# Second layer of a two-layer mixture of experts: one weight conversion behind the low halves, the second job's place lookup behind its next half of products

## The chip, the cores and the metric

The kernel runs on one core of one Trainium2 chip. The metric is device time in microseconds of the whole program, the median of the runs. In the profile the engines are PE (TensorE matrix products), PEld (its weight loads), DVE (VectorE), ACT (ScalarE), POOL (GpSimd) and SP (SyncE, here the queue of the weight loads).

## The reference

A retention layer (blockwise attention with decay) gives 1536 tokens of 512 values. Two mixtures of experts follow, each with 8 experts of 512 -> 1024 -> 512. The first sends every token to two experts with noisy gates; the second, which the change touches, to one:

```python
logits = x @ w_gate
expert_idx = np.argmax(logits, axis=1)
...
for i in range(N):
    e = expert_idx[i]
    if counts[e] < capacity:
        disp[e, counts[e]] = x[i]
        pos[i] = counts[e]
        counts[e] += 1
        keep[i] = True
h = np.maximum(np.einsum('ecd,edf->ecf', disp, w1), 0.0)
y = np.einsum('ecf,efd->ecd', h, w2)
for i in range(N):
    if keep[i]:
        out[i] = gate_w[i] * y[expert_idx[i], pos[i]]
```

Here the capacity is 384 and everything is float32.

## The kernel before

Each layer is a list of jobs. A job is an expert with a number of token places: the second layer has a first job S of 256 places and a second job T of 128 places for the same expert (the largest), then the other experts by size, the next one with 336 places. For a job the tokens' rows are gathered from DRAM by POOL (L529, indirect DMA), POOL adds their two parts (the join, L540), PE transposes them (L860), ACT and DVE split them into a high and a low half (L861, L862), and PE multiplies.

A float32 product is made of three products of halves (`three`, L870 to L872): high x high, high x low, low x high. So every weight part of 128 x 1024 is converted too: ACT makes the high half (L108, `convert`), DVE the low half (L114, `convert_low`), after which its landing buffer is free for the next load from SP (`places`). The converted parts stand in rings of four for each matrix.

Job T has only 128 places, so it is worked "by token" in four steps (`steps`): two halves of the first product (`first_rows`; ACT's relu at L979 follows each), then the transposed activations of a half (`turn`: PE at L987, ACT's high half at L990, DVE's low half at L991) and the second product. The first half of the second product is `highs_first` (L1024), which takes all products with high halves before those with low halves; the rest is `second` (L870 to L872). `turn(0)` is recorded inside `first_rows(1)`, `turn(1)` inside step 2.

For every place the kernel must also know its gate weight and its target row. `one_hot` finds them with products of a one-hot matrix (L402), a copy (L404), a transposition (L407) and some small DVE operations (L408 to L426: `far` L424, the weight `wt` L426, the target `dst` L425). For S and T the first two columns are looked up early and the rest by `rest()`, named `jobS.rest` and `jobT.rest`; the ranked lookup for all later jobs is `later[1][7]` (L483, L505). The outputs of a job are scaled by the weight (ACT at L1110, DVE at L1108) and scattered (L1117).

`experts` walks through jobs and steps. After each step it records what runs beside it: conversions, the next job's gather and split (`nxt.ready()`), and `extra2(j, i)`, hand-written work for job j, step i. `sooner` lists the steps at which `extra2` comes ahead of the conversions. The order of each engine's instructions is made from this recording and from `tc.issue_after(...)`, which orders an instruction behind a named one; `tail` holds the last instruction of a kind. At job 1 (T):

```python
if j == 1 and i == 0:
    with tc.issue_after(tail["pe"]):
        jobS.rest()
        later[1][7]()
    places.append(more[2])
if j == 1 and i == 1:
    with tc.issue_after(tail["pe"]):
        jobT.rest()
    with tc.issue_after(tail["dve"]):
        st2 = sizes_by_expert(...)
        later.append(leftovers(...))
```

`leftovers` counts the tokens that found no place (L1187 to L1197, with `sizes_by_expert` at L361 to L367); a branch four jobs later reads the count.

Of the kernel before, what the change touches and what calls it, by code (L numbers as in the profile page):

```python
# [8 lines left out]
F32 = mybir.dt.float32  # L9
# [28 lines left out]
def kernel(ctx: ExitStack, tc: tile.TileContext, q, k, v, lam, g1, gn, noise,  # L38
                                  w1, w2, g2, u1, u2, capacity, out):
    nc = tc.nc  # L40
    B, H, S, D = q.shape
    T, DM = out.shape
    E, _, F = w1.shape
# [20 lines left out]
    def bank(tag, shape, dt=F32):  # L64
        bufs = 2 if tag in ("hp", "tr") else 1
        return psum.tile(shape, dt, name=tag, bufs=bufs)
# [6 lines left out]
    tail = {}  # L73
# [9 lines left out]
    def fetch():  # L83
        if not wq or not places:
            return
        key, layer, j, src = wq.pop(0)
        st = places.pop(0)
        if layer == 0:
            a = src[:, j * 256:(j + 1) * 256].rearrange("(c p) f -> p c f", p=P)
            i = nc.sync.dma_start(st.rearrange("p (c f) -> p c f", c=DC), a)  # L90
        else:
            a = src[j * 256:(j + 1) * 256, :].rearrange("(c p) d -> p c d", p=P)
            i = nc.sync.dma_start(st.rearrange("p (c d) -> p c d", c=2), a)
        tail["sp"] = i.ins
        while hold:
            tc.add_manual_dep(i.ins, hold.pop().name, mybir.DependencyInfo(
                mybir.DependencyClass.Sync, mybir.DependencyReason.DATA), reason="loads behind a gather")
        staged.append((key, layer, j, st))

    def convert():  # L100

        if not staged or split_[staged[0][1]] - used[staged[0][1]] == RING:
            return
        key, layer, j, st = staged.pop(0)
        at = split_[layer] % RING
        hi, lo = wh[layer][at], wl[layer][at]
        split_[layer] += 1
        tail["cast"] = nc.scalar.copy(hi, st).ins  # L108
        lows.append(((key, layer, j), hi, lo, st))

    def convert_low():
        if lows:
            part, hi, lo, st = lows.pop(0)
            tail["low"] = nc.vector.tensor_sub(lo, st, hi.bitcast(F32)).ins  # L114
            wparts[part] = (hi, lo)
            places.append(st)
# [40 lines left out]
    i = nc.sync.dma_start(lam1, lam.rearrange("(o h) -> o h", o=1))  # L157
# [25 lines left out]
    ps = bank("yp3", [P, H])  # L183
# [690 lines left out]
    class Job:  # L874
# [107 lines left out]
        def turn(self, m, ahead):  # L982
            r = self.rows
            ps = bank("tr", [P, 4, P])[:, :, :r]
            with tc.issue_after(ahead):
                for i in range(4):
                    nc.tensor.transpose(ps[:, i, :], self.h["r", m][:r, i * P:(i + 1) * P], ident[:r, :r])  # L987
            t = work.tile([P, 2, 512], F32R, name="h", bufs=3).rearrange("p a (b c) -> p a b c", b=4)[:, :, :, :r]
            hh, hl = t[:, 0], t[:, 1]
            nc.scalar.copy(hh, ps)  # L990
            nc.vector.tensor_sub(hl, ps, hh.bitcast(F32))  # L991
            for i in range(4):
                self.h[4 * m + i] = t[:, :, i, :]

# [130 lines left out]
    def experts(jobs, last, extra=None, count=None, between=None, joins=3, sooner=()):  # L1125

        j = 0
        tail.pop("both", None)
        while j < len(jobs) and j != count:
            job = jobs[j]  # L1130
            steps = job.steps()
            for i, step in enumerate(steps):
                for _ in range(0 if job.quiet else 2 if len(steps) == 4 else 1):
                    fetch()
                if job.pairs and i == 1:
                    convert_low()
                step()
                nxt = jobs[j + 1] if j + 1 < len(jobs) else None
                if i == len(steps) - 1 and j + 1 < len(jobs) and j + 1 != count:
                    job.collect()  # L1140
                if i == job.clears and last is not None:
                    last.collect()
                    last.finish()
                    if j == 0 and between is not None:
                        between()
                if i == 1 and nxt is not None:
                    nxt.prepare()
                if nxt is not None and i >= (1 if job.by_token else joins):
                    nxt.join()
                if i == 6 and j + 2 < len(jobs) and nxt.by_token:  # L1150
                    jobs[j + 2].prepare()
                tail.pop("cast", None)
                tail.pop("low", None)
                sooner_cast = nxt is not None and nxt.pairs and job.by_token and i == 2
                if sooner_cast:
                    with tc.issue_after(tail["act"]):
                        convert()
                if i == len(steps) - 2 and nxt is not None:
                    nxt.ready()
                if extra is not None and (j, i) in sooner:  # L1160
                    extra(j, i)
                with tc.issue_after(tail["act"]), tc.issue_after(tail["dve"]):
                    if job.pairs or sooner_cast:
                        while lows:
                            convert_low()
                    for _ in range((2, 2, 0 if sooner_cast else 1, 1)[i] if job.by_token else (2, 1, 1, 1, 1, 1, 1, 0, 0)[i] if job.pairs
                                   else 2 if i < 4 else 1):
                        convert()
                        if not job.pairs:
                            convert_low()  # L1170
                if job.later is not None:
                    with ExitStack() as order:
                        for x in ("act", "dve", "cast", "low"):
                            if x in tail:
                                order.enter_context(tc.issue_after(tail[x]))
                        job.later()
                    job.later = None
                if extra is not None and (j, i) not in sooner:
                    extra(j, i)
            last = job  # L1180
            j += 1
        return last
# [270 lines left out]
    def ahead():  # L1453
# [15 lines left out]
        jobs.append(jobS)  # L1469

    last = experts(jobs, None, extra1, count=len(FIRST) + 2)
    total, body = over1
    with tc.If(total > 0):  # L1473
# [85 lines left out]
    def extra2(j, i):  # L1559
        if j == 0 and i == 2:  # L1560
            route2()
            jobT.src, jobT.dst, jobT.wt, jobT.rest, _, picked = one_hot("D", keyB, aux2, *BEHIND, False, "yp2")
            jobT.g = gather(jobT.src, jobT.n, jobT.rows, x2_rows)
            jobT.join()
            later.append(picked)
        if j == 0 and i == 3:
            with tc.issue_after(later[0]):
                later.append(others())
                jobS.quiet = True
                of, _, pick, spread1, mark = later[1][:5]  # L1570
                pick()
                spread1()
                mark(range(NT))
        if j == 0 and i == 7:
            with tc.issue_after(tail["pe"]):
                later.append(later[1][5]())
                for r in TURNS:
                    jobs.append(Job(("b", r), SECOND[r], later[1][0](r), x2_rows, out, False, SECOND[r][1] > 1, True))
                jobs[2].prepare()
            hold.append(brought[-2])  # L1580
        if j == 0 and i == 7:
            with tc.issue_after(later[3]), tc.issue_after(tail["dve"]):
                gates()
                later[1][6]()
        if j == 1 and i == 0:
            with tc.issue_after(tail["pe"]):
                jobS.rest()
                later[1][7]()
            places.append(more[2])
        if j == 1 and i == 1:  # L1590
            with tc.issue_after(tail["pe"]):
                jobT.rest()
            with tc.issue_after(tail["dve"]):
                st2 = sizes_by_expert("b", later[2], [n for n, _ in SECOND] + [BEHIND[0]])
                later.append(leftovers("b", tab2, table2_full, tot2, st2, x2_rows, u1, u2, out, False))

    jobL = last
    last = experts(jobs, jobL, extra2, count=BEFORE + 2, between=lambda: all_logits(jobL), sooner=((1, 0),))
    def settle(j, i):

# [7 lines left out]
    with tc.If(total > 0):  # L1608
        body()
    last = experts(jobs[BEFORE + 2:], last, settle)  # L1610
    last.collect()
    last.finish()
# [34 lines left out]
```

## Time and profile before

| | |
|---|---|
| median of 3 runs | 598.44 us (598.14 to 599.72) |
| the profiled execution | 600.24 us, its span 598.6 us |
| PE busy | 585.1 us, 98% of the span |
| DVE, ACT, POOL busy | 372.5, 279.8, 182.5 us |
| granted TensorE clock, mean | 0.998 |

Times in the rows are microseconds from the start of the span. A busy PE is not a PE at its peak, since products are pipelined: a product's row is longer than the distance to the next one. Job T lies between 436 and 455 us.

### The profile page before, as it was taken

The numbers are of one execution on the slowest core, as the hardware profiler recorded it, in microseconds if no ns is written. First come the engines' busy times: TensorE is split into PE (matmuls) and PEld (weight loads), VectorE is DVE, ScalarE is ACT, GpSimd is POOL, SyncE is SP. The second block draws the span as 40 slices with busy tenths as digits, with TensorE's granted clock in tenths as the row PEclk, the third lists the DMA queues.
The fourth block names the chain that finished last, engine by engine and source line by source line (L and its number), as shares of the span: only waits on it lengthen the run. The fifth ranks groups of instructions, "written<-read, shape, count | busy, mean of one in ns | idle before, by whom it ended". The sixth has DMA issues, their size and how long they took to land. (4 is left out here: it accounts for less than half of the span.)

```text
span 598.6 us, 11608 instructions
## 1 busy us (share of the span) xinstructions
PE 585.1 (98%) x4305; PEld 555.3 (93%) x4305; DVE 372.5 (62%) x858; ACT 279.8 (47%) x488; POOL 182.5 (30%) x256
## 2 busy tenths in 40 slices
PE   8998989999999999999999999999999999999996
PEld 7997889989999999999999999998879999998996
DVE  5467789766363464543644556546887567667893
ACT  3565530354353343433434435037137367467782
POOL 4965500416023041050130501033165334331204
PEclk9999999999999999999999999999999999999999
DMA  9999415248545357377453520291289967956841
GB/s 183 267 281 264 119 64 190 78 133 298 193 150 185 107 180 229 103 249 211 132 189 105 199 84 30 64 321 61 72 284 338 328 220 217 351 184 215 273 146 35
DMA packets 104869, 109.76 MB, mean 183 GB/s; under 512 B 35700, under 2 KB 80756, under 8 KB 104803
## 3 DMA queue, kind: packets, MB, share of 16 engines
q1 hardware_dynamic: 96722, 83.05, 46.1%
q0 software_dynamic: 8080, 25.88, 12.4%
q8 instruction: 36, 0.59, 0.4%
q14 instruction: 31, 0.25, 0.1%
HBM read 91.89 MB, written 18.71 MB: 185 GB/s over the span
## 5 line engine op out<-in xcount | busy, mean ns | idle before, releaser
L114 DVE TENSOR_TENSOR wl<-wst,wh 128x1024 fp32r<-128x1024 f32 x107 | 134.7, 1267 | 54.6 <-ACT wh L108 49.4
L108 ACT CAST wh<-wst 128x1024 fp32r<-128x1024 f32 x107 | 111.4, 1048 | 33.4 <-PE yp L871 21.8
L870 PE MATMUL hp<-x,wh 128*128 128x364 f32 (+9 forms) x352 | 116.0, 330 | 0.8 <-ACTq L1473 0.4
L871 PE MATMUL hp<-x,wh 128*128 128x364 f32 (+9 forms) x352 | 115.8, 329 | 0.0
L872 PE MATMUL hp<-x,wl 128*128 128x364 f32 (+9 forms) x352 | 114.9, 327 | 0.0
L958 ACT ACTIVATE h<-hp 128x364 fp32r<-128x364 f32 (+9 forms) x88 | 41.2, 468 | 156.2 <-PE hp L872 143.2
L870 PE MATMUL yp<-h,wh 128*128 128x364 f32 (+8 forms) x320 | 106.1, 333 | 0.0
L872 PE MATMUL yp<-h,wl 128*128 128x364 f32 (+8 forms) x320 | 106.0, 332 | 0.0
L871 PE MATMUL yp<-h,wh 128*128 128x364 f32 (+8 forms) x320 | 105.3, 329 | 0.0
L959 DVE SCALAR_TENSOR_TENSOR h<-hp,h 128x364 fp32r<-128x364 f32 (+9 forms) x88 | 46.3, 526 | 60.7 <-ACT h L958 57.5
L1117 POOL DMA_INDIRECT x<-y,Rdst x25 | 24.7, 987 | 176.7 <-DVE y L1091 173.1
L870 PEld LDWEIGHTS hp<-x,wh 128*128 128x128 f32 x352 | 66.1, 188 | 2.0 <-ACTq L1473 0.8
L871 PEld LDWEIGHTS hp<-x,wh 128*128 128x128 f32 x352 | 66.1, 188 | 0.7 <-DVE x L1271 0.2
L872 PEld LDWEIGHTS hp<-x,wl 128*128 128x128 f32 x352 | 66.1, 188 | 0.0
L871 PEld LDWEIGHTS yp<-h,wh 128*128 128x128 f32 x320 | 60.2, 188 | 0.2 <-DVE h L959 0.2
L870 PEld LDWEIGHTS yp<-h,wh 128*128 128x128 f32 x320 | 60.0, 188 | 0.3 <-issue 0.2
L872 PEld LDWEIGHTS yp<-h,wl 128*128 128x128 f32 x320 | 60.1, 188 | 0.0
L862 DVE TENSOR_TENSOR x<-tr,x 128x128 fp32r<-128x128 f32 (+11 forms) x68 | 27.3, 434 | 26.7 <-ACT x L861 25.8
L861 ACT CAST x<-tr 128x128 fp32r<-128x128 f32 (+11 forms) x68 | 24.4, 386 | 32.5 <-PE tr L860 30.2
L540 POOL TENSOR_TENSOR xg<-xg 128x512 f32<-128x512 f32 (+1 forms) x16 | 23.5, 1469 | 43.2 <-DMA xg<-x,Tsrc 28.9
L529 POOL DMA_INDIRECT xg<-x,Rsrc x25 | 29.0, 1158 | 18.4 <-DVE Rsrc L497 11.1
L1082 PE MATMUL tr<-iw,yT 128*128 128x136 f32 (+3 forms) x224 | 34.3, 288 | 0.1
(391 smaller groups left out, 1037.7 us busy)
## 6 DMA issues: line engine op xcount, KB each, us to landing
wst<-in_moe_w_dram SPq DMA_DIRECT2D x107, 512.0 KB
more<-in_moe_w_dram SPq DMA_DIRECT2D x21, 512.0 KB
ldk<-in_k_dram SPq DMA_DIRECT2D x12, 256.0 KB
ldv<-in_v_dram SPq DMA_DIRECT2D x12, 256.0 KB
x<-xr SPq DMA_DIRECT2D x12, 256.0 KB
out_dram<-zero SPq DMA_DIRECT2D x12, 256.0 KB
ldq<-in_q_dram SPq DMA_DIRECT2D x5, 512.0 KB
ldq<-in_q_dram SPq DMA_DIRECT2D x2, 256.0 KB
```

What stands on the lines that cost most here:

```text
L108: tail["cast"] = nc.scalar.copy(hi, st).ins
L114: tail["low"] = nc.vector.tensor_sub(lo, st, hi.bitcast(F32)).ins
L529: i = nc.gpsimd.indirect_dma_start(out=r, out_offset=None, in_=x, in_offset=bass.IndirectOffsetOnAxis(ap=src(s)[:m], axis=0))
L861: a = nc.scalar.copy(hi[:, d, :n], ps[:, :n])
L862: v_ = nc.vector.tensor_sub(lo[:, d, :n], ps[:, :n], hi[:, d, :n].bitcast(F32))
L870: nc.tensor.matmul(ps, a[0], b[0], start=start, stop=False)
L871: nc.tensor.matmul(ps, a[0], b[1], start=False, stop=False)
L872: tail["pe"] = nc.tensor.matmul(ps, a[1], b[0], start=False, stop=stop).ins
L958: tail["act"] = nc.scalar.activation(hh, ps, AF.Relu).ins
L959: tail["dve"] = nc.vector.scalar_tensor_tensor(hl, ps, 0.0, hh.bitcast(F32), op0=OP.max, op1=OP.subtract).ins
L1082: nc.tensor.matmul(ps[:m, i, :], self.yT[:, 2 * b + i, s * r:s * r + m], iw[:, 2 * b + i, gates2], start=True, stop=True)
L1117: i = nc.gpsimd.indirect_dma_start(out=target, out_offset=bass.IndirectOffsetOnAxis(ap=dst, axis=0), in_=y, in_offset=None, bounds_check=t ...
```

## The change

Three edits, all for the second job of the second layer:

```diff
@@ turn
-            nc.vector.tensor_sub(hl, ps, hh.bitcast(F32))
+            tail["low_h"] = nc.vector.tensor_sub(hl, ps, hh.bitcast(F32)).ins
@@ experts
                 tail.pop("low", None)
+                if (j, i - 1) in sooner:
+                    tail["dve"] = tail["low_h"]
...
-                    for _ in range((2, 2, 0 if sooner_cast else 1, 1)[i] if job.by_token else (2, 1, 1, 1, 1, 1, 1, 0, 0)[i] if job.pairs
-                                   else 2 if i < 4 else 1):
+                    casts = ((2, 2, 0 if sooner_cast else 1, 1)[i] if job.by_token else (2, 1, 1, 1, 1, 1, 1, 0, 0)[i] if job.pairs
+                             else 2 if i < 4 else 1)
+                    for c in range(casts):
                         convert()
-                        if not job.pairs:
+                        if not job.pairs and not (c and (j, i) in sooner):
                             convert_low()
@@ extra2
-        if j == 1 and i == 1:
+        if j == 1 and i == 2:
             with tc.issue_after(tail["pe"]):
                 jobT.rest()
+        if j == 1 and i == 1:
             with tc.issue_after(tail["dve"]):
                 st2 = sizes_by_expert("b", later[2], [n for n, _ in SECOND] + [BEHIND[0]])
```

The only step in `sooner` is (1, 0), the first step of job T in the second layer. At that step the low half of the second conversion is no longer recorded. At step 1 `tail["dve"]` is set to the low halves of `turn(0)`, and the conversion's low half and the leftover counts are recorded behind them. `jobT.rest()` moves from step 1 to step 2. The number of instructions is the same on every engine, and SP's queue has the same order. Lines behind L1151 have numbers that are two to four higher after the change.

**DVE, in job T.** The piece from the copy of S's lookup (L404) on; `wl_84` is the low half of the second conversion, `blw` and `bli` belong to the leftover counts, `y` is S's scaled output. Before:

```order
L404 COPY tabi<-tr 4x256
L114 TENSOR_TENSOR wl_84<-wst_73,wh_76 128x1024
L408 COPY Soa<-tr 128x2x4
L505 TENSOR_REDUCE Twt<-yp_5281 128x21
L424 TENSOR_SCALAR Sfar<-Soa 128x2
L426 TENSOR_REDUCE Swt<-Soa 128x2
L1193 TENSOR_REDUCE blw<-blw 128x1
L425 TENSOR_TENSOR Sdst<-Stok,Sfar 128x2
L1197 CAST bli<-blw 128x18
L991 TENSOR_TENSOR h<-tr,h 128x512
L1108 TENSOR_SCALAR y<-yp_4868,Swt 128x512
```

After:

```order
L404 COPY tabi<-tr 4x256
L505 TENSOR_REDUCE Twt<-yp_5281 128x21
L408 COPY Soa<-tr 128x2x4
L424 TENSOR_SCALAR Sfar<-Soa 128x2
L426 TENSOR_REDUCE Swt<-Soa 128x2
L425 TENSOR_TENSOR Sdst<-Stok,Sfar 128x2
L1108 TENSOR_SCALAR y<-yp_4868,Swt 128x512
L991 TENSOR_TENSOR h<-tr,h 128x512
L114 TENSOR_TENSOR wl_84<-wst_73,wh_76 128x1024
L361 MEMSET bsv 128x1 x8
```

The conversion stood between L404 and everything that makes S's weight; now it stands behind the low halves (L991), and the leftover counts, which began among the gate operations earlier, follow it.

**PE, in job T.** The piece around the first products of the second half (L1024); `yp_5349`, `yp_5363` and `ohs` belong to T's lookup. Before:

```order
L402 LDWEIGHTS aux_160
L402 MATMUL yp_5349<-ohs,aux_160 4x128
L1024 MATMUL yp_5403<-wh_79,h 128x512
L407 MATMUL yp_5363<-iw,tabi 128x4
L1024 MATMUL yp_5403<-wl_87,h 128x512
L1024 MATMUL yp_5403<-wh_79,h 128x512
L1024 MATMUL yp_5403<-wl_87,h 128x512
L1024 MATMUL yp_5403<-wh_79,h 128x512 x2
L987 MATMUL tr<-iw,hr 128x128 x4
```

After, the L1024 follow the last product of `first_rows` directly, then L987 and this piece, where `yp_5430` is T's lookup and `xg` are the next job's gathered rows:

```order
L870 MATMUL yp_5383<-wh_80,h 128x512
L871 MATMUL yp_5383<-wl_88,h 128x512
L872 MATMUL yp_5383<-wh_80,h 128x512
L870 MATMUL yp_5383<-wh_80,h 128x512
L871 MATMUL yp_5383<-wl_88,h 128x512
L872 MATMUL yp_5383<-wh_80,h 128x512
L860 MATMUL tr<-iw,xg 128x128 x2
L860 MATMUL tr<-iw,xg 128x80
L860 MATMUL tr<-iw,xg 128x128 x2
L860 MATMUL tr<-iw,xg 128x80
L402 LDWEIGHTS aux_160
L402 MATMUL yp_5430<-ohs,aux_160 4x128
```

T's lookup (twelve L402 and L407) went from ahead of and between the L1024 to behind the first two sets of the next job's transpositions.

**POOL, in job T.** One piece of the difference; `Tsrc` are places of the next jobs, `Sdst` the targets of S:

```order
 L529 DMA xg<-x_67,Tsrc 80x1104
 L540 TENSOR_TENSOR xg<-xg 128x4x128 x2
-L540 TENSOR_TENSOR xg<-xg 80x4x128
-L529 DMA xg<-x_67,Tsrc 128x1104
 L1117 DMA out_dram<-y,Sdst 1536x512 x2
+L540 TENSOR_TENSOR xg<-xg 80x4x128
+L529 DMA xg<-x_67,Tsrc 128x1104
 L540 TENSOR_TENSOR xg<-xg 128x4x128
 L529 DMA xg<-x_67,Tsrc 128x1104 x2
```

The two scatters of S now come ahead of the join of the next job's third tile (80 rows) and of a further gather. On ACT the one row that moves is L1110, the scaling of S's output: it now stands ahead of the first L990 instead of behind it.

## Rows read from the trace of the kernel before

**Rows 1.** The page: busy time of each engine, its share of the span, instructions.
```profile
PE 585.1 (98%) x4305; PEld 555.3 (93%) x4305; DVE 372.5 (62%) x858; ACT 279.8 (47%) x488; POOL 182.5 (30%) x256
```

**Rows 2.** Waits of PE from 400 us on: total us, times, longest us.
```profile
PE yp L1024 <- ACT y L1110: 0.6, 1, 0.6
PE yp L407 <- DVE tabi L404: 0.5, 1, 0.5
```

**Rows 3.** Timeline of PE: start us, us, instruction, idle before and its releaser.
```profile
445.10 0.83 PE L402 MATMUL yp<-ohs,aux 128*4 128x128 bf16 x12
446.55 0.50 PE L1024 MATMUL yp<-wh,h 128*128 128x512 f32 x1 [0.62 <-ACT y L1110]
447.55 0.22 PE L407 MATMUL yp<-iw,tabi 4*128 4x4 f32 x1 [0.49 <-DVE tabi L404]
447.70 0.50 PE L1024 MATMUL yp<-wl,h 128*128 128x512 f32 x1
...
450.81 0.75 PE L860 MATMUL tr<-iw,xg 128*128 128x128 f32 x6
...
452.37 0.47 PE L860 MATMUL tr<-iw,xg 128*128 128x128 f32 x3
...
454.67 0.40 PE L872 MATMUL yp<-wh,h 128*128 128x512 f32 x1
454.90 0.32 PE L870 MATMUL hp<-x,wh 128*128 128x336 f32 x1
```

**Rows 4.** Timeline of POOL, 442 to 452 us (columns as above).
```profile
442.17 1.30 POOL L540 TENSOR_TENSOR xg<-xg 128x512 f32<-128x512 f32 x1
443.88 1.82 POOL L540 TENSOR_TENSOR xg<-xg 128x512 f32<-128x512 f32 x1 [0.41 <-DMA xg<-x,Tsrc]
446.49 1.27 POOL L540 TENSOR_TENSOR xg<-xg 80x512 f32<-80x512 f32 x1 [0.79 <-DMA xg<-x,Tsrc]
...
449.18 1.02 POOL L1117 DMA_INDIRECT out_dram<-y,Sdst  x1 [0.30 <-issue]
450.50 1.01 POOL L1117 DMA_INDIRECT out_dram<-y,Sdst  x1 [0.30 <-issue]
```

**Rows 5.** Timeline of DVE, 437 to 453 us.
```profile
437.65 0.22 DVE L363 TENSOR_TENSOR bse<-brk,e_up 128x64 f32<-128x64 f32 x1
...
441.94 2.62 DVE L114 TENSOR_TENSOR wl<-wst,wh 128x1024 fp32r<-128x1024 f32 x1 [0.26 <-ACT wh L108]
...
444.69 1.03 DVE L424 TENSOR_SCALAR Sfar<-Soa 128x2 f32<-128x2 f32 x1
...
445.97 0.68 DVE L991 TENSOR_TENSOR h<-tr,h 128x512 fp32r<-128x512 f32 x1
...
451.77 0.92 DVE L862 TENSOR_TENSOR x<-tr,x 128x336 fp32r<-128x336 f32 x2 [0.79 <-ACT x L861]
```

**Rows 6.** Timeline of ACT, 443 to 452 us.
```profile
443.85 0.59 ACT L990 CAST h<-tr 128x512 fp32r<-128x512 f32 x1 [1.95 <-PE tr L987]
445.81 0.69 ACT L1110 ACTIVATE y<-yp,Swt 128x512 f32<-128x512 f32 x1 [1.37 <-DVE Swt L426]
...
451.30 0.78 ACT L861 CAST x<-tr 128x336 fp32r<-128x336 f32 x2 [1.04 <-PE yp L872]
```

**Rows 7.** Timeline of POOL, 533 to 535 us, a scatter behind a join.
```profile
533.12 1.29 POOL L540 TENSOR_TENSOR xg<-xg 80x512 f32<-80x512 f32 x1 [3.09 <-DMA xg<-x,Tsrc]
534.57 1.82 POOL L1117 DMA_INDIRECT out_dram<-y,Tdst  x1 [0.16 <-issue]
```

**Rows 8.** Timeline of DVE, 534 us, beside that scatter.
```profile
534.25 1.25 DVE L114 TENSOR_TENSOR wl<-wst,wh 128x1024 fp32r<-128x1024 f32 x1 [0.31 <-ACT wh L108]
```

**Rows 9.** Timeline of POOL, 460 us, a gather that starts ahead of a conversion.
```profile
460.82 0.96 POOL L529 DMA_INDIRECT xg<-x,Tsrc  x1 [0.30 <-issue]
```

**Rows 10.** Timeline of DVE, 461 us, the conversion beside it.
```profile
461.13 1.21 DVE L114 TENSOR_TENSOR wl<-more,wh 128x1024 fp32r<-128x1024 f32 x1
```

**Rows 11.** Timeline of SP's queue, 447 us, a weight load.
```profile
447.83 0.38 SPq L93 DMA_DIRECT2D wst<-in_moe_w_dram  x1
```

## The prediction

> **What bounds the kernel now.** I read the page first: PE is busy 98% of the span [rows 1], so only a PE idle stretch can be won, and work moved on other engines counts only where PE waits for it. The view of PE's waits comes next. From 400 us on it names two waits at the jobs that the change touches, and both lie within a microsecond of each other [rows 2]. The timeline of PE shows the place: the second job's place lookup (twelve small L402) ends at 445.93; then the first product of its second half (L1024) waits 0.62 us for ACT's scaling of the first job's output, and the lookup's transposition (L407) waits 0.49 us for DVE's copy [rows 3]. The product pitch is 0.23 us (454.67 to 454.90), so L407 at 447.55, where it could have followed L1024 by 0.23, costs 447.55 - 446.55 - 0.23 = 0.77. **Together the two stalls cost 1.4 us.**
>
> Why ACT and DVE are late stands in the DVE timeline: the second weight conversion runs 2.62 us from 441.94 because POOL's join holds it up, and the weight column of the first job's outputs waits behind it; the next join then stretches L424 to 1.03 us [rows 4, 5]. Only then can ACT scale (445.81) [rows 6].
>
> **The change, part by part.** No instruction is added or removed on any engine.
>
> *The second conversion moves behind the low halves (L991).* L424 and what follows it need no longer wait for 2.62 us of conversion. Even if L424 now meets the first join (442.17, 1.30 us [rows 4]), it ends near 443.6, ACT scales until about 444.3, and the high halves follow by 0.59 [rows 6]. PE reaches L1024 near 445.1, since the lookup ahead of it is gone. First stall: gone, 0.62. The conversion itself then starts when L991 (0.68 us [rows 5]) is done: about 445.1 if L424 slips in before the join, about 445.7 if it doesn't. The weight buffer that it frees was free at 444.56 and will be at about 446.9; the load into it may be the one at 447.83 [rows 11], and is not later in either case. I cost this at nothing.
>
> *The second job's lookup moves behind its next half of products.* L407 no longer stands between the products of the second half, and DVE copies for it while PE has other work. Second stall: gone, 0.77. Its cover is the rest of that half: three L402, a product and three transpositions. The job's scaled output is wanted only after the next job has begun, so the later lookup holds up nobody.
>
> *The leftover counts go behind the conversion on DVE.* These are nine short operations of about 0.2 us [rows 5] and nine memsets; their result is used four jobs later. But the second L991 and the splits of the next job's rows (L862) stand behind them.
>
> *What is late next: POOL.* This is where I expect the gain to go. Ahead of the next job PE transposes its gathered rows (L860). Before, all three joins were done by 446.49 + 1.27 = 447.76, and PE came at 450.81, three microseconds later [rows 3, 4]. Now PE comes earlier by the stalls (1.4), by the lookup (0.83) and by L407 (0.15): about 448.4. And the third join now stands behind the first job's two scatters. The second join cannot start before 443.88, because it waited there for its gather's data. So the third ends at 443.88 + 1.30 + gap 0.16 + scatter 1.02 + gap 0.30 + scatter 1.01 + 1.27 = **448.94 at the earliest** [rows 4, 7]. Its rows are the third of the first three transpositions, near 448.6. PE waits at least 0.3 us.
>
> After this join the second pair of transposition banks follows as before: from 450.81 to 452.37 is 1.56 us for two sets of three, from the third transposition on about 1.4. PE had four products in that time; now it has nine small L402, so about 0.5 us of idle PE appears. From there to the next job's first product took 2.53 us with eight products [rows 3]; now there are twelve (4 x 0.23 more), L407 (0.15), three L402 (0.2) and the changes between small and large products, about 3.9. The next job therefore starts 1.4 + 3.9 = 5.3 us after the third join; before, it started at 454.90.
>
> - Join ends at 448.94 (no scatter held up): 454.25, **0.65 us sooner**.
> - One scatter held up by the conversion, as at 534.57 (1.82 in place of 1.02): join at 449.74, start at 455.05, **0.15 later**.
> [...]
>
> Whether the scatter is held up depends on who starts first. A gather that began 0.31 us ahead of a conversion ran its normal 0.96 [rows 9, 10]; the scatter that began 0.32 after one took 1.82 [rows 7, 8]. Here the first scatter comes at 443.88 + 1.30 + 0.16 = 445.34, in the middle of the conversion's 445.1 to 445.7, and the second at 446.66, in the conversion's last quarter if that came second. I take the middle case, one scatter held up: +0.15, rounded to +0.2.
>
> [...]
>
> **The sum.** The profiled execution took 600.24 us (span 598.6); with +0.2 it becomes 600.4. It stands 1.8 us above the median of the runs shown (598.44), to which the same +0.2 is carried: **598.6 us**. About 0.3% (1.8 us) is what a measurement of this kernel can tell from no change.
>
> **The rivals.**
>
> 1. *Both stalls go and nothing takes their place.* POOL's spans are rough, and the join might not bind. Then -1.4: 597.0. For it: PE shows no other wait here [rows 2]. Against it: the second join waited for data until 443.88, and two scatters can't take under 2 us. Chance 0.17.
> 2. *No scatter is held up by the conversion:* -0.65, 597.8. [...] Against it: rows 7 and 8. Chance 0.17.
> 3. [...] Chance 0.2.
> 4. *The change only renames the wait:* ACT now scales before it copies the high halves, so L1024 waits for the copy instead, by 0.69 + 0.59 [rows 6] from a late weight column. If L424 is held up as before, L1024 comes at about 445.1 to 446; this shortens the wait at the join by as much, so the end stays where the join puts it: 598.4 to 598.6. Chance 0.06.
>
> **How the numbers follow.** The forecast (one scatter held up, within 0.3 of +0.2) has 0.40. All cases lie between 597.0 and 599.6, inside 0.3%. The three runs shown reach from 598.14 to 599.72, so I add a little of that scatter at the ends: 596.9 to 600.0. Faster by over 0.3% needs more than the whole of both stalls: 0.04. Slower by over 0.3% needs rival 3 and more: 0.05. Within 0.3%: 0.91.
>
> **What would show it.** Right: the two waits of rows 2 are gone; PE has a wait at L860 for a POOL join (L540) of 0.3 to 1.5 us and a second one there for DVE's L862; the 80-row join ends at 449 to 450; the next job's first product lies at 454.2 to 455.6, and everything behind it is shifted alike. Wrong: the next job starts before 454.0 (then POOL didn't bind), or after 456 (then DVE holds it), or PE has new waits for weights in the jobs after it, which I exclude because SP's loads keep their order.

## The result, and the profile after

The changed kernel takes **603.13 us** (median of 7 runs, 600.49 to 604.11) against 598.99 us for the kernel before (7 runs): ratio **1.0068, interval 1.0057 to 1.0079**, slower by 0.68%. In a later series of runs it was 604.09 against 599.63 us, 1.0065 [1.0043, 1.0087]. The forecast was 598.6, the range 596.9 to 600.0: wrong.

The profiled execution took 604.11 us, its span 602.4. On the page nothing is left out and nothing new is done; PE is 98% busy as before [rows 1], only for 3.3 us longer:

```profile
PE 588.4 (98%) x4305; PEld 557.8 (93%) x4305; DVE 375.6 (62%) x858; ACT 279.8 (46%) x488; POOL 180.6 (30%) x256
```

PE's waits from 400 us on, in the changed kernel: the two of rows 2 are gone, and one for POOL's join has come.

```profile
PE tr L860 <- POOL xg L540: 1.9, 1, 1.9
...
PE tr L860 <- DVE x L862: 0.2, 1, 0.2
```

All of job T lies 0.65 us earlier in this execution than in the one before (its first gather of the next job's rows starts at 436.14 instead of 436.79), so I compare distances from that gather. Timeline of PE, the columns of rows 3:

```profile
444.37 0.40 PE L1024 MATMUL yp<-wh,h 128*128 128x512 f32 x1
...
447.60 0.38 PE L860 MATMUL tr<-iw,xg 128*128 128x128 f32 x2
449.93 0.58 PE L860 MATMUL tr<-iw,xg 80*128 80x80 f32 x4 [1.95 <-POOL xg L540]
450.44 0.66 PE L402 MATMUL yp<-ohs,aux 128*4 128x128 bf16 x9
451.28 0.63 PE L860 MATMUL tr<-iw,xg 128*128 128x128 f32 x3 [0.18 <-DVE x L862]
...
454.75 0.63 PE L870 MATMUL yp<-wh,h 128*128 128x512 f32 x1
455.18 0.63 PE L871 MATMUL yp<-wl,h 128*128 128x512 f32 x1
...
458.17 0.48 PE L872 MATMUL yp<-wh,h 128*128 128x512 f32 x1
458.48 0.32 PE L870 MATMUL hp<-x,wh 128*128 128x336 f32 x1
```

Two things are to be seen. PE transposes two tiles, then idles 1.95 us for the third. And behind that wait the same products come every 0.43 us (454.75 to 455.18) instead of every 0.23 [rows 3]. The next job begins at 458.48, **22.34 us** after the first gather; before, it was 454.90 - 436.79 = **18.11**.

The timeline of POOL says why the third tile is late, and that of DVE what held the scatter:

```profile
443.98 1.30 POOL L540 TENSOR_TENSOR xg<-xg 128x512 f32<-128x512 f32 x1 [2.02 <-DMA xg<-x,Tsrc]
445.44 1.81 POOL L1117 DMA_INDIRECT out_dram<-y,Sdst  x1 [0.17 <-issue]
447.56 1.01 POOL L1117 DMA_INDIRECT out_dram<-y,Sdst  x1 [0.30 <-DVE blw L1197]
448.57 1.29 POOL L540 TENSOR_TENSOR xg<-xg 80x512 f32<-80x512 f32 x1
```

```profile
444.44 1.93 DVE L114 TENSOR_TENSOR wl<-wst,wh 128x1024 fp32r<-128x1024 f32 x1
```

The second join waits for its gather's data, the first scatter takes 1.81 us beside the conversion, the second 1.01, and only then comes the join of 80 rows, until 449.86. This is the chain the prediction described: the conversion ends at 446.37 and the scatter that started beside it 0.88 us later, as at 534 us (0.89 [rows 7, 8]).

What it did not describe stands in the windows. Changed kernel, then the kernel before; the column behind the busy times is PEclk, the granted clock as a share of full speed:

```profile
448.00:452.00 4.00, 1.89 (x18) 1.34 (x19) 1.66 (x6) 0.83 (x3) 2.86 (x3) 0.94 0.97 284
452.00:456.00 4.00, 4.00 (x13) 2.89 (x12) 2.51 (x8) 2.72 (x4) 0.00 (x0) 0.50 1.03 399
456.00:460.00 4.00, 4.00 (x17) 3.44 (x16) 1.42 (x2) 0.69 (x1) 2.09 (x2) 0.71 1.01 309
```

```profile
448.00:452.00 4.00, 4.00 (x24) 3.32 (x23) 1.27 (x5) 1.29 (x3) 2.90 (x3) 1.00 1.01 322
452.00:456.00 4.00, 4.00 (x25) 3.38 (x24) 2.85 (x5) 3.08 (x6) 0.00 (x0) 1.00 1.02 368
456.00:460.00 4.00, 4.00 (x28) 4.00 (x28) 3.29 (x5) 3.35 (x6) 3.79 (x2) 1.00 0.96 338
```

Before, the clock is whole in these windows. Now it drops to 0.50 behind the wait. The time lost by it is the sum of what is missing from 1: 4 x 0.06 + 4 x 0.50 + 4 x 0.29 = **3.4 us**. The rest of the local loss of 22.34 - 18.11 = 4.23, 0.8 us, is about what PE waits more: 1.95 + 0.18 instead of 0.62 + 0.49. Six of the seven runs had a mean clock of 0.993 or 0.994; the seventh, at 0.999, took 600.49, still 1.5 us above the median of the kernel before.

### The profile page after: what moved, and what is told of

It reads as the page before. It is cut to its first block, busy times and chain, and to the rows that moved or that the text cites. A ratio compares the mean times of both kernels' runs of the same rounds, so it can differ in the third digit from the quotient of the medians.

```text
span 602.4 us, 11605 instructions
## 1 busy us (share of the span) xinstructions
PE 588.4 (98%) x4305; PEld 557.8 (93%) x4305; DVE 375.6 (62%) x858; ACT 279.8 (46%) x488; POOL 180.6 (30%) x256
## 5 line engine op out<-in xcount | busy, mean ns | idle before, releaser
L870 PE MATMUL hp<-x,wh 128*128 128x364 f32 (+9 forms) x352 | 116.0, 330 | 0.8 <-ACTq L1476 0.4
L871 PE MATMUL hp<-x,wh 128*128 128x364 f32 (+9 forms) x352 | 115.8, 329 | 0.0
L870 PE MATMUL yp<-h,wh 128*128 128x364 f32 (+8 forms) x320 | 106.1, 333 | 0.0
L871 PE MATMUL yp<-h,wh 128*128 128x364 f32 (+8 forms) x320 | 105.4, 330 | 0.0
L870 PEld LDWEIGHTS hp<-x,wh 128*128 128x128 f32 x352 | 66.1, 188 | 2.1 <-ACTq L1476 0.8
L871 PEld LDWEIGHTS hp<-x,wh 128*128 128x128 f32 x352 | 66.1, 188 | 0.7 <-DVE x L1274 0.2
L871 PEld LDWEIGHTS yp<-h,wh 128*128 128x128 f32 x320 | 60.2, 188 | 0.4 <-DVE h L959 0.4
L870 PEld LDWEIGHTS yp<-h,wh 128*128 128x128 f32 x320 | 60.0, 188 | 0.3 <-issue 0.2
```

Source lines behind the costliest of these rows:

```text
L870: nc.tensor.matmul(ps, a[0], b[0], start=start, stop=False)
L871: nc.tensor.matmul(ps, a[0], b[1], start=False, stop=False)
```

## The experiments

Two theories stood against each other: the time goes with **the clock**, which falls behind the new wait; or it goes with **the waits themselves** and with DVE and POOL holding each other up. Ratios are against runs of the kernel before in the same series; the experiments came in three series on three chips (e1 to e4; e5 to e7 and the kernel before again; e8, e9, e7 again and the changed kernel again), on which it took 599.02, 601.79 and 599.63 us. "Distance" is from the first gather of the next job's rows to that job's first product, in the profiled execution; the clock is that of 452 to 456 us, where job T's second half runs. The mean clock of a run, where it is named, also counts a fall at the end of the program: in the profile of the kernel before the clock is 1.00 up to 595 us and 0.68 from there on, where PE has no more work, and the mean is 0.998.

| kernel | PE's waits in job T, us | distance | clock | ratio |
|---|---|---|---|---|
| before (two profiles) | 0.62, 0.49 | 18.11, 18.11 | 1.00 | |
| changed (two profiles) | 1.95 and 1.80 at the join, 0.18 | 22.34, 22.19 | 0.50 | 1.0068, 1.0065 |
| e1 join first | 0.77 | 17.96 | 1.00 | 1.0016 [1.0003, 1.0029] |
| e2 lookup alone | none | 16.88 | 1.00 | 0.9992 [0.9978, 1.0006] |
| e3 conversion alone | 0.76, 0.16, 0.92 | 19.18 | 1.00 | 1.0020 [1.0008, 1.0033] |
| e4 wait filled, 8 products | none | 19.37 | 1.00 | 1.0024 [1.0011, 1.0036] |
| e5 wait without the conversion | 1.86 | 18.98 | 1.00 | 1.0026 [1.0011, 1.0041] |
| e6 one scatter ahead | 1.16 | 18.50 | 1.00 | 1.0031 [1.0007, 1.0055] |
| e7 join first, counts later | 0.37; none | 17.15, 16.73 | 1.00 | 0.9981 [0.9967, 0.9996], 0.9986 [0.9977, 0.9995] |
| e8 longer wait | 3.10 | 23.21 | 0.62 | 1.0079 [1.0055, 1.0103] |
| e9 wait filled, 4 products | none | 18.12 | 1.00 | 1.0006 [0.9996, 1.0017] |

**e1, the third join ahead of S's scatters.** The changed kernel; on POOL alone the third join goes back ahead of the two scatters. The further gather, which before also stood ahead of them, stays behind them.

```diff
@@ scatter
-        i = nc.gpsimd.indirect_dma_start(out=target, out_offset=bass.IndirectOffsetOnAxis(ap=dst, axis=0),
...
+        with tc.issue_after(tail["ahead"]) if "ahead" in tail else ExitStack():
+            i = nc.gpsimd.indirect_dma_start(out=target, out_offset=bass.IndirectOffsetOnAxis(ap=dst, axis=0),
...
@@ experts, ahead of last.finish()
+                if (j, i - 1) in sooner:
+                    nxt.join()
+                    tail["ahead"] = tail["both"]
```

> The changed kernel with one thing turned round on POOL: the third join stands ahead of the first job's two scatters, as before the change; all other engines keep the changed order. Theory C (the join makes PE wait about 2 us, and after that the granted clock is 0.50 for about 7 us): the wait at the row transposition is under 0.3 us, the granted clock is 1.00 from 440 to 462 us, and the time falls by both, to 597.0 to 598.5 us, that is 0.5 to 1.5 us faster than the kernel before. Theory W (the loss lies in the later lookup and the leftover counts on DVE, which keep the next job's rows waiting): the join's wait goes, another takes its place, and the time stays at 600 us or above.

Measured: 600.29 us. The wait at the join is gone and so is the fall of the clock in job T, 2.8 us of the loss. But e1 is not faster than before: C was right about the clock and missed the time, which is the one that W named, 600 or above. Its PE waits elsewhere, for a transposition bank that DVE frees late; first PE, then POOL, then DVE:

```profile
450.44 0.51 PE L860 MATMUL tr<-iw,xg 128*128 128x128 f32 x3 [0.77 <-DVE h L991]
```

```profile
445.10 3.53 POOL L540 TENSOR_TENSOR xg<-xg 128x512 f32<-128x512 f32 x2 [1.59 <-DMA xg<-x,Tsrc]
```

```profile
447.52 1.19 DVE L363 TENSOR_TENSOR bse<-brk,e_up 128x64 f32<-128x64 f32 x1
```

An operation of 64 columns, the first of the leftover counts, takes 1.19 us instead of 0.22 [rows 5] while two joins run, and L991 stands behind it.

**e2, the lookup alone.** Only `jobT.rest()` is moved; conversion, counts and POOL as before.

> The kernel before with the second job's lookup moved and nothing else; the conversion stays where it was and POOL keeps its order. Theory C: the wait for the scaled output grows by what the lookup covered (0.6 to about 1.4 us), the wait at the lookup's transposition (0.5) goes, no wait at the row transposition; if an idle stretch of 1.4 us leaves the clock at 1.00, the time is that of before within 0.5 us; if it halves the clock, 2 to 4 us slower. Theory W: slower by 1 us or more with the clock at 1.00.

Measured: 599.01 us. Locally it wins 18.11 - 16.88 = 1.23 us, nearly the 1.4 that the prediction gave both stalls, and PE has no wait in job T, where a longer wait for the scaled output was expected. Not all of this need be the lookup's: in this execution the conversion, which the edit leaves alone, took 1.20 us instead of 2.62 [rows 5]. In the whole program the gain is too small for these runs.

**e3, the conversion and the counts alone.** `jobT.rest()` stays at step 1.

> The kernel before with the conversion moved and nothing else; the lookup stays, and POOL has the scatters ahead of the third join. Theory C: the two old waits go, PE comes to the row transposition about 1 us later than with the whole change and waits there for POOL about 1 us; if that is short enough for the clock to stay at 1.00, the time is 598 to 599 us, within 0.5 us of before; if it halves the clock, 601 to 603. Theory W: as much slower as the whole change, whatever the clock does.

Measured: 600.61 us, between what the two theories named, so both missed it. It is the conversion's part that loses. PE, then DVE:

```profile
446.92 0.22 PE L407 MATMUL yp<-iw,tabi 4*128 4x4 f32 x1 [0.76 <-DVE bsv L361]
...
451.45 0.51 PE L860 MATMUL tr<-iw,xg 128*128 128x128 f32 x3 [0.92 <-DVE h L991]
```

```profile
444.41 2.25 DVE L114 TENSOR_TENSOR wl<-wst,wh 128x1024 fp32r<-128x1024 f32 x1
446.59 0.27 DVE L404 COPY tabi<-yp 4x128 f32<-4x128 f32 x1
...
448.40 1.81 DVE L1190 TENSOR_TENSOR ov<-cnt,bst 128x8 f32<-128x8 f32 x1
```

The copy for L407 stands behind the conversion, and an eight-column operation of the counts runs 1.81 us, from beside the second scatter to the end of the third join (450.19), with L991 behind it. But none of the waits reaches a microsecond, and the clock stays whole.

**e4 and e9, the wait filled.** The changed kernel with products of zeros, read by nobody, on PE ahead of the transpositions; e9 has `range(4)`.

```diff
@@ experts, ahead of nxt.ready()
+                if (j, i - 2) in sooner:
+                    with tc.issue_after(tail["pe"]):
+                        for _ in range(8):
+                            tail["pe"] = nc.tensor.matmul(bank("yp3", [P, P]), zero, zero, start=True, stop=True).ins
```

> The whole change with eight unread 128x128 products of zeros added on PE ahead of the row transpositions, where it waits for POOL's join; POOL's order and the join's time stay. Theory C, the clock's share: PE is busy in most of the wait, the granted clock stays at 1.00, the next job starts when the join lets it, and the time is 599 to 600.5 us, 2.5 to 4 us faster than the whole change though PE has more to do. Rival (the clock falls for another reason than the idle stretch, or costs little): 602.5 us or more.

> The changed kernel with 4 products of zeros, which nobody reads, on PE ahead of the next job's transpositions, in place of 8: 8 took 4.05 us, so 4 take 2.0, and the transpositions start when they do in the changed kernel (about 449.9) but without an idle stretch. Theory (of the loss against the kernel before, most is the clock): no fall behind it, mean clock as in the kernel before, next job's first product about 3.4 us sooner than in the changed kernel's profile, median 2 to 3 us below the changed kernel in this call. Rival (the loss is the wait itself): the time stays within 1 us of the changed kernel.

Measured: e4 600.85 us, e9 599.89 us. PE has *more* to do than in the changed kernel and is done 2.3 and 4.2 us sooner (603.13 and, in e9's series, 604.09). e4 misses its range by 0.35: its eight products lie in 447.63 to 451.68, longer than the wait. In e9 the zeros, and two of job T's products that come between them (L870 and L871), last about as long as the wait did, and the transpositions start 450.65 - 437.32 = 13.33 us after the first gather (changed: 449.93 - 436.14 = 13.79):

```profile
448.79 0.38 PE L1163 MATMUL yp<-zero 128*128 128x128 f32 x2
448.93 0.48 PE L870 MATMUL yp<-wh,h 128*128 128x512 f32 x1
449.24 1.02 PE L1163 MATMUL yp<-zero 128*128 128x128 f32 x4
450.02 0.48 PE L871 MATMUL yp<-wl,h 128*128 128x512 f32 x1
450.33 0.48 PE L1163 MATMUL yp<-zero 128*128 128x128 f32 x2
450.65 0.74 PE L860 MATMUL tr<-iw,xg 128*128 128x128 f32 x6
...
455.44 0.32 PE L870 MATMUL hp<-x,wh 128*128 128x336 f32 x1
```

```profile
452.00:456.00 4.00, 4.00 (x24) 3.31 (x22) 3.29 (x11) 2.99 (x5) 0.00 (x0) 1.00 1.04 392
```

POOL is nearly as late in e9 as in the changed kernel: its held scatter took 1.81 us too, and its third join ended 13.22 us after the first gather, where the two profiles of the changed kernel have 13.72 and 13.59. But PE doesn't stand still, and the clock stays whole. From the first of these transpositions on, the next job is 4.79 us away instead of 458.48 - 449.93 = 8.55; the two products that moved into the wait are 0.46 of the difference of 3.76, and the clock's 3.4 us the rest to within 0.1. This is the experiment that decides what the wait at the join costs. In the medians the loss against the kernel before is gone, 1.0006, an interval that holds 1; among runs with a like clock e9 stands about 1 us above the kernel before, which comes up again at the end of the next section.

**e5 and e8, a wait without the moved conversion.** Lookup moved as in e2, conversion and counts as before; the third join goes behind S's scatters and behind one added join (e8: two) on values that are no longer needed.

```diff
@@ both
+            with tc.issue_after(tail["behind"]) if k == 2 and "behind" in tail else ExitStack():
+                if k == 2 and "behind" in tail:
+                    spent = g[1][:, ROW:ROW + DC * W].rearrange("p (d w) -> p d w", w=W)[:, :, :P]
+                    tail["behind"] = nc.gpsimd.tensor_add(spent, spent, spent).ins
+            with tc.issue_after(tail["behind"]) if k == 2 and "behind" in tail else ExitStack():
+                tail["both"] = nc.gpsimd.tensor_add(a, a, b).ins
...
@@ experts, ahead of nxt.join()
+                if (j, i - 1) in sooner:
+                    tail["behind"] = tail["scatter"]
```

> Only the lookup is moved (as in the run with the lookup alone: no wait of PE in job T, next job 16.88 us after the first gather of its rows, 599.01 us), the conversion and the counts stay as in the kernel before, and POOL's third join is delayed without them: it stands behind S's two scatters and behind one added join of 128 rows whose result nobody reads. From the lookup-alone trace: second join ends 444.2, scatters 444.4 to 445.4 and 445.7 to 446.7, added join to 448.1, third join to about 449.4, PE there at 447.6: idle for about 1.8 us. Theory (an idle of this length at this place lowers the granted clock, whatever makes it): the clock falls to 0.5 for several us behind the wait, the next job starts 5 us later than with the lookup alone, 602.5 to 604.0. Rival (the clock fell because of the moved conversion or the work around it): clock stays at 1.00, only the wait is paid, 600.3 to 601.2.

> As the run with the idle stretch alone (lookup moved, conversion and counts as before, third join behind both scatters and behind added joins that nobody reads), with two added joins in place of one: the idle stretch should be about 1.86 + 1.07 = 2.9 us in place of 1.86. Theory (an idle stretch of PE at this place lowers the clock in a share of the executions, the longer the stretch the more of them): nearly every run at a mean clock of 0.994 or lower, median 2.5 to 4.5 us above the run with 1.86 us. Rival (the falls have nothing to do with this stretch): the same mix of clocks as with one added join, median 1.0 us above it.

Measured: e5 603.19 us beside 601.79 of before, e8 605.35 beside 599.63. In e5's profiled execution PE waits 1.86 us at the same place, and **the clock does not fall**:

```profile
450.73 0.58 PE L865 MATMUL tr<-iw,xg 80*128 80x80 f32 x4 [1.86 <-POOL xg L545]
```

```profile
452.00:456.00 4.00, 4.00 (x23) 3.28 (x21) 3.28 (x11) 2.67 (x4) 0.00 (x0) 1.00 1.05 402
```

There the wait costs about its own length: the distance is 18.98, 2.1 us more than in e2. So the theory's forecast for e5 missed for this execution. That the median lies in its range is luck: the range was worked out for another chip, on which the kernel before is 2.8 us faster, and 1.4 us above the kernel before is what the rival named (600.3 to 601.2, beside 599.02). Its ten runs lie apart: five at a mean clock of 0.998 (600.97 to 602.91 us), five at 0.992 to 0.997 (603.47 to 604.36). Where the clock fell in those five is not shown, and the kernel before has such runs too (15 of 25 at 0.995 to 0.997). In e8, with 3.10 us, it falls in the profile, and three of four runs have a mean of 0.991:

```profile
452.10 0.58 PE L866 MATMUL tr<-iw,xg 80*128 80x80 f32 x4 [3.10 <-POOL xg L546]
```

```profile
452.00:456.00 4.00, 3.90 (x25) 3.10 (x26) 1.34 (x5) 1.56 (x5) 1.04 (x2) 0.62 1.05 397
456.00:460.00 4.00, 4.00 (x10) 3.09 (x11) 3.43 (x8) 1.98 (x3) 0.83 (x1) 0.53 0.57 216
```

The loss is again 4 x 0.38 + 4 x 0.47 = 3.4 us. No conversion was moved here, so the fall (to 0.62 and 0.53) does not need one.

**e6, one scatter ahead of the join, the other behind.** The changed kernel; the second scatter is kept back and issued behind `nxt.join()`.

> The changed kernel with only one of S's two scatters ahead of the third join, the second behind it. The join should then run from about 447.4 to 448.7 in place of 449.86, and PE should wait about 0.8 us there instead of 1.95. Theory (the clock's fall hangs on the long idle; the shorter one is paid once): clock 1.00 in 440 to 462 us, 599.5 to 600.5. Rival (any wait for the join at this place costs the clock): a fall behind it, 601.5 to 603. Rival (the scatter isn't the delay): the join still ends near 449.8 and the time stays at 603.

Measured: 603.62 us beside 601.79, above the 599.5 to 600.5 expected. A miss in its particulars, too. The join runs from 447.32 as expected and PE no longer waits for it; but now it starts while the counts are under way. One of them, begun at 446.70 beside the end of the scatter, ends only behind the join, at 448.70, and PE waits for DVE instead. PE, POOL, DVE:

```profile
450.11 0.51 PE L861 MATMUL tr<-iw,xg 128*128 128x128 f32 x3 [1.16 <-DVE h L992]
```

```profile
447.32 1.29 POOL L541 TENSOR_TENSOR xg<-xg 80x512 f32<-80x512 f32 x1
```

```profile
446.70 2.00 DVE L365 TENSOR_TENSOR bse<-bse,bsv 128x64 f32<-128x64 f32 x1
```

The profiled execution (600.91 us) has the whole clock in job T. Five of ten runs have a mean of 0.994 or less and take 604.51 to 606.17; none of the 25 of the kernel before is as low. That the shorter wait costs the clock in those is not shown.

**e7, the join first and the counts behind the second L991.** e1 with one more edit, against the 0.77 us left in it. Run in two series.

```diff
@@ extra2
-        if j == 1 and i == 1:
-            with tc.issue_after(tail["dve"]):
+        if j == 1 and i == 2:
+            with tc.issue_after(tail["low_h"]):
                 st2 = sizes_by_expert("b", later[2], [n for n, _ in SECOND] + [BEHIND[0]])
```

> The changed kernel with the third join ahead of the scatters (measured 600.29) and in addition the leftover counts behind the second low halves (L991) on DVE instead of ahead of them. Theory (what is left of the loss there is DVE: one of the counts is held up 1.0 us beside a join, L991 and L862 come late, and PE waits 0.77 us for a transposition bank): that wait goes, 599.0 to 599.6. Rival (the rest of the loss comes from the conversion itself or from elsewhere): 600.0 to 600.5 with the wait still there.

> The version with the third join ahead of the scatters and the leftover counts behind the second low halves again, with more rounds, on the chip of this call: it measured 0.9981 [0.9967, 0.9996] of the kernel before. Theory (its job T is 0.96 us shorter and has one wait of 0.37 us): again 0.997 to 0.9995, the interval below 1. Rival (that was a matter of the runs): 0.9995 to 1.001.

Measured: 600.38 beside 601.79 us, and with more rounds 598.82 beside 599.63 us. **By the medians this version beats both kernels**, the one before by 0.14% [0.05, 0.23] in the larger sample. That job T's shorter distance makes this gain is not shown: in the larger sample ten of e7's eleven runs have a mean clock of 0.998 or more, but only six of 21 of the kernel before, and these have nearly the same median, 598.68 and 598.54. So the gain there goes with fewer runs at a lower clock, and why they are fewer is open. In the other series the runs of that clock do differ: 600.24 (7 of 10) against 601.11 (10 of 25). PE in the second profile goes through without a wait:

```profile
447.66 0.74 PE L860 MATMUL tr<-iw,xg 128*128 128x128 f32 x6
448.34 0.83 PE L402 MATMUL yp<-ohs,aux 128*4 128x128 bf16 x12
...
452.93 0.32 PE L870 MATMUL hp<-x,wh 128*128 128x336 f32 x1
```

**The two kernels again.** The kernel before, profiled a second time, and the changed kernel in the last series.

> The kernel before, unchanged, profiled a second time, since its first profile stands 1.8 us above its median and every local comparison leans on it. Theory: the local distance from the first gather of the next job's rows to that job's first product is again near 18.1 us, with the two waits of 0.6 and 0.5 us. Rival: it is shorter (about 17.3), which would explain why the changed kernels lose 0.8 us more in the whole than locally.

> The changed kernel, unchanged, beside the other kernels of this call on the same chip. Theory (the fall behind the wait of 1.95 us comes in most executions, not in all): most runs at a mean clock 0.004 to 0.006 below the kernel before, the rest at its clock and about 1 to 2 us above it; median 0.5 to 0.9% above the kernel before. Rival (the falls were a matter of the first chip): clocks as in the kernel before, median at most 0.35% above.

The kernel before has the same distance, 18.11, and the same two waits (0.62 and 0.50), so rows 2 and 3 were no accident of one execution. The changed kernel waited 1.80 us, and its clock fell again, at about 451.5 us; of its four runs three have a mean of 0.993 or 0.994, one 0.995. The falls are not a matter of one chip either: the profiles show them in this series and, near 50 us, in e1, whose chip was another.

## Why the prediction was wrong

- **Both old stalls go: right.** L1024 and L407 wait for nothing any more, and with that rival 4 falls. By parts, the conversion alone (e3) ends only the first wait, as forecast; the lookup alone (e2) ends both, but with the shorter conversion named there, so its share is not shown.
- **POOL is what is late next, and one scatter is held up: right.** The first scatter took 1.81 us beside the conversion, the second 1.01 without it; rows 7 and 8 gave 1.82 beside one, rows 4 1.02 and 1.01. Rivals 1 and 2 fall with this.
- **The time from the third join to the next job, "1.4 + 3.9 = 5.3 us": the step that failed.** It carried the pitch of 0.23 us from rows 3 past a wait, as if PE came out of it at the same speed. Measured: 449.93 to 458.48, 8.55 us. With the clock whole the working was good: e9 took 455.44 - 450.65 = 4.79 with two products already behind it, so 4.79 + 2 x 0.23 = 5.25. The missing 3.3 us are the clock's, whose fall (to 0.50 in 452 to 456 us) cost 3.4 by the windows. The prediction had no term, no bound and no rival for it; PE's idle time was priced at its own length everywhere. Of its signs of being wrong one came, a next job after 456 (458.48), but not with the reason named there, DVE.
- **The wait itself: named, but mis-sized.** 0.3 to 1.5 us were forecast, 1.95 and 1.80 measured. PE came when expected: the third transposition could start about 11.8 us after the first gather (448.6 - 436.79), and it could at 447.98 - 436.14 = 11.84. The join was late: forecast at 449.74 - 436.79 = 12.95, measured 13.72. The second join waited for its gather until 7.84 us after the first gather began, where I had taken 443.88 - 436.79 = 7.09 as fixed. In e6 and e9 it was 7.06 and 7.32.
- **Rival 3, the slower case of 599.6: not in this kernel.** Why DVE and POOL should make each other late, on which its +0.5 and +0.7 rest, is shown by no run; what is shown are lengths side by side. In the changed kernel the conversion starts ahead of the scatter (444.44 and 445.44), the scatter takes 1.81 us, and the counts are nearly through when the third join starts (448.57). In e1, e3 and e6 a join runs beside one of the counts, which takes 1.19, 1.81 and 2.00 us, and PE waits 0.77, 0.92 and 1.16 us for DVE.
- **The sum without the clock: of the right kind, too small by about 0.6.** Less the clock's 3.4 us the distances of the changed kernel are 18.94 and 18.79, that is 0.8 and 0.7 us more than before; 0.15 was forecast, and the late join makes the difference. In job T the clock has 3.4 of the 4.2 us lost. e9's distance of 18.12, that of before, is a little less than this sum, since its join came 0.5 us sooner and two products moved into the wait.

What stays open: why six of the changed kernel's seven runs have a mean clock of 0.993 or 0.994, its profile falling to 0.50 behind a wait of 1.95 us, while e5's profiled execution keeps 1.00 behind one of 1.86 us; and why e1 and e2 stand 1.1 and 0.7 us higher in the whole program than their distances say (e1: 0.16% of 599 us is 0.96, its distance 0.15 shorter). e9 does so too, where runs of a like clock are compared: at a mean of 0.998 or more six of its ten runs have a median of 599.69 us, six of 21 of the kernel before 598.54, and the distances are 18.12 and 18.11. For the changed kernel the clock's 3.4 and the 0.7 to 0.8 us of longer waits come to about what the medians of the whole program lose, 4.1 to 4.5 us.

## What to carry to other kernels

Price an idle stretch of the engine that sets the time twice: once at its length, and once at what a lower clock would take from the work behind it; here that was 3.4 us for a wait of 1.95, and nothing in e5's profile for one of 1.86, so it is a chance times a cost. When work is moved, look at what the scheduler then puts first on the slower queue: two scatters ahead of one short addition made this loss, and the addition put first, with small two-input DVE operations kept from running beside it (1.19 to 2.00 us beside a join in e1, e3 and e6, 0.16 to 0.29 where none ran), took the loss away (e7, 600.38 beside 601.79 us). A wait filled with worthless products shows whether it is the wait or the clock that costs, if the trace is then read for what else moved (here two products of job T). And before a small gain by medians is put down to an edit, compare runs of a like clock.

## What the runs showed of the hardware

- The clock fell not in the wait but after it: PE resumed at 449.93, the clock was still whole at 451 and at 0.50 from about 451.5 to 458.3 us, though PE worked without a pause in those 7 us.
- The same idle stretch doesn't always do it. Every profiled execution here has one near 47 to 49 us, of 2.29 us (1.99 in the first of e7). Behind it the clock fell in those of e1, e8 and e9 (0.88 over 46 to 60 us), and in none of the other eleven (1.00). PE's timeline and two windows of e1, and those windows of the kernel before:

```profile
49.84 0.19 PE L319 MATMUL yp<-mbA,tri 128*128 128x6 bf16 x1 [2.29 <-DVE mbA L732]
```

```profile
46.00:50.00 4.00, 1.71 (x38) 1.45 (x35) 3.66 (x11) 1.53 (x2) 2.12 (x2) 0.94 1.05 277
50.00:54.00 4.00, 3.93 (x26) 3.73 (x24) 2.66 (x11) 1.56 (x4) 0.00 (x0) 0.64 0.65 179
```

```profile
46.00:50.00 4.00, 1.71 (x25) 1.52 (x24) 3.77 (x9) 0.81 (x2) 1.82 (x2) 1.00 1.07 293
50.00:54.00 4.00, 3.93 (x51) 3.62 (x51) 2.00 (x11) 3.33 (x7) 1.99 (x3) 1.00 1.01 299
```

  There it cost 4 x 0.06 + 4 x 0.36 = 1.7 us. A median over runs of such a kernel can mix both: of the changed kernel's seven runs six have a mean of 0.993 or 0.994, one 0.999.
- A DVE multiplication of 128 x 64 values (L365, in e6) took 2.00 us, from 446.70 to 448.70, beside the end of a scatter (447.29) and a POOL join of 1.29 us, and 0.22 in the changed kernel, where no join ran beside it.
